# The written-out order of a gated recurrence with a convolutional gate, chosen anew

## The chip, the cores and the metric

The kernel runs on one core of a Trainium2 chip. The core has five engines with a queue each: TensorE (PE; its weight loads are listed as PEld), VectorE (DVE), ScalarE (ACT), GpSimd (POOL) and SyncE (SP), which here only issues transfers. The time is that of one execution on the device, in microseconds (us); lower is better.

## The reference

Four sequences of 6336 tokens with 256 channels go through a linear recurrence with gates, and its result `y` through a unit whose gate is a causal convolution over five tokens. Cut to what matters:

```python
sig_r, sig_i = sigmoid(r_gate), sigmoid(i_gate)
a_t = exp(8.0 * sig_r * log(clip(sigmoid(a_param), 1e-6, 1 - 1e-6)))
x_gated = sqrt(max(1.0 - a_t * a_t, 1e-6)) * sig_i * x
for t in range(S):
    h = a_t[:, t] * h + x_gated[:, t]
    y[:, t] = h
gate = sigmoid(sum(conv_w[k] * shifted(y, 4 - k) for k in range(5)))
out = (gate * (y @ w_val)) @ w_out
```

All inputs and the output are float32 in HBM.

## The kernel before

The 25344 tokens are cut into 50 windows of 512 tokens (the last has 256), and the windows into 27 chunks: chunks 0, 1 and 25 are one window of 512, chunk 26 one of 256, the others two windows each. Thus chunk c from 2 to 24 is windows 2(c-1) and 2(c-1)+1; window 48 is chunk 25, window 49 chunk 26. A half of a chunk is 128 of the 256 channels.

Each step is a small function named `op_` and two letters, and a table calls it by those letters. `ORDER` (from line 42) is one long string of such words: name, number of the window or chunk, half, and behind `@` the PSUM banks. The kernel walks through it once and emits the instructions; each engine runs its own in the order in which they come in the string, and waits in place where an input or a buffer isn't there. So the string alone fixes all queues, including SP's, on which all large transfers stand.

The words, by engine, with the line of the profile:

- SP: `lr`, `li`, `lx` load a window of r_gate, i_gate and x (L284); `st` stores a window of the output (L533); `s_wl` loads parts of the weights (L258 to L264).
- ACT: `ta`, `tb` the tangents (tanh) of a chunk of r and i (L302, L305); `ex` the exponential that makes the decays `aring` of a half (L365); `rt` the square roots of part of a batch of chunks (L398); `tg` the tangent for the gate of a window (L489); `ca` a copy of a window's result from PSUM (L522); `sa` a square (L381). Exponential and square root need different tables, and a change of table is a load on ACT (L549); `rt` come in pairs for each of eight batches, the first two batches in one go.
- POOL: `sq` the squares of the decays of a half (L373); `pp` adds one to a window of tangents (L312); `up` multiplies it with x (L324).
- DVE: `xg` multiplies with the square roots (L423, from chunk 24 on L427); `sc` the scan, that is the recurrence of a half (L470); `gv` the product of gate and value (L502); `cd` a copy of a window's result (L520); `uv` does for a window what `pp` and `up` do on POOL (L338), from x that `xp` brought to PSUM.
- PE: `tr` transposes the tangents of r (L349), `nt` the square roots (L412), `xt` the scan's input (L437); `cv` the convolution (L482), `vl` the value product (L497), `ou` the output product (L512), `xp` (L329).

A window's way is lr, ta, tr, ex, sq, rt, nt, and li, tb, pp, lx, up beside it, then xg, xt, sc, cv, tg, vl, gv, ou, a copy (ca or cd) and st. From chunk 24 on xt comes ahead of xg, and the scan reads the product from SBUF and not from PSUM: there both inputs of the scan, and both of `up`, lie in SBUF. The rings hold a few windows: four of r, i and x, so that lr.4 must wait until ta.0 has read window 0; and the eight PSUM banks are given to the steps by the words themselves. `ta` of two neighbouring chunks is transposed together (`tr` and `ex` of chunks 2, 4, 6 and so on treat that chunk and the next).

Of the kernel before, what the change touches and what calls it, by code (L numbers as in the profile page):

```python
# [47 lines left out]
lx.6 tr.4.1@2,3 tg.0 li.8 pp.5 sc.1.1 tr.4.0@4,5 ta.6 li.9 xt.2.1@7 pp.4 sc.2.1 vl.0@0,1 up.4 ex.4.0 gv.0 nt.3@6,7 up.5
ex.4.1 xt.2.0@5 cv.1@0,1 sc.2.0 sq.5.0 tb.4 ou.0.0@2,3 xg.3 vl.1@4,5 tg.1 sq.4.1 li.10 cd.0.0 xt.3.0@7 lx.9 ta.7 lr.15
cv.2@0,1 gv.1 li.11 sq.4.0 tg.2 sc.3.0 lr.17 tr.6.0@2,3 xt.3.1@4 lx.8 ex.6.0 sq.5.1 lr.14 cv.3@0,1 sc.3.1 tb.5 pp.6  # L50
tr.6.1@6,7 up.6 xp.7@2,3 uv.7 ex.6.1 li.12 lx.11 ou.1.0@4,5 cd.1.0 sq.7.0 lx.10 tg.3 st.0 xp.9@2,3 uv.9 tb.6 cv.4@0,1
sq.6.0 tg.4 li.14 vl.2@2,3 sq.6.1 li.13 gv.2 lr.16 vl.3@0,1 li.15 lx.13 gv.3 rt.2.0 vl.4@4,5 pp.8 ou.2.0@2,3 gv.4
sq.7.1 ou.3.0@0,1 cd.3.0 up.8 rt.2.1 cd.2.0 nt.4@0,1 xg.4 pp.10 lx.12 ou.4.0@2,3 st.2 pp.11 cd.4.0 xt.4.0@0 up.11
sc.4.0 nt.5@2,3 tb.7 xt.4.1@6 cv.5@4,5 up.10 lx.15 xg.5 st.1 ta.9 sc.4.1 xt.5.0@0 pp.12 nt.6@2,3 ta.8 lr.20 pp.13 lr.21
xg.6 up.13 vl.5@6,7 tb.8 lr.19 sc.5.0 lr.18 tr.8.0@2,3 li.16 xt.5.1@1 lx.14 tg.5 pp.15 li.17 li.18 ex.8.0 gv.5 up.15
st.3 tr.8.1@4,5 li.19 sc.5.1 ou.5.0@6,7 st.4 ex.8.1 up.12 nt.7@2,3 xt.6.1@0 cd.5.0 ta.11 cv.8@4,5 sq.8.1 sc.6.1 st.5
cv.6@6,7 tg.8 pp.14 tg.6 xg.7 vl.6@4,5 ta.10 sq.9.0 cv.7@0,1 gv.6 xt.6.0@7 tg.7 up.14 lr.23 sc.6.0 ou.6.0@4,5 lr.22
tb.9 lx.19 tr.10.0@0,1 lx.17 sq.9.1 vl.7@2,3 cd.6.0 ex.10.0 xt.7.0@7 gv.7 st.6 sq.8.0 vl.8@4,5 lx.18 tb.10 li.21
cv.9@0,1 gv.8 lx.16 sq.11.0 sc.7.0 tg.9 tr.10.1@2,3 li.23 ex.10.1 ou.7.0@4,5 pp.17 ou.8.0@0,1 cd.7.0 pp.16 xt.7.1@7
ta.12 cv.10@2,3 sq.10.1 cd.8.0 st.7 li.20 cv.11@4,5 lr.24 sc.7.1 tg.10 st.8 sq.10.0 lr.25 tg.11 vl.10@2,3 lr.27 gv.10  # L60
sq.11.1 vl.9@0,1 li.22 rt.3.0 gv.9 ou.10.0@6,7 up.17 cd.10.0 vl.11@2,3 cv.12@4,5 gv.11 pp.19 lx.21 rt.3.1 lr.26
ou.9.0@0,1 up.19 cd.9.0 nt.8@6,7 xg.8 st.9 ou.11.0@0,1 st.10 up.16 cd.11.0 xt.8.0@6 sc.8.0 nt.10@0,1 pp.18 tg.12 lx.20
xt.8.1@2 tb.11 up.18 sc.8.1 nt.9@6,7 ta.13 cv.13@4,5 pp.21 xg.9 pp.20 tg.13 lr.29 tr.12.1@2,3 xg.10 xt.9.1@6 lr.28
up.21 ex.12.1 li.25 cv.14@4,5 sc.9.1 lx.22 lx.23 li.24 vl.12@0,1 tg.14 sq.13.1 vl.13@2,3 tb.12 gv.12 tr.12.0@6,7
sq.12.1 gv.13 vl.14@4,5 ex.12.0 li.27 gv.14 lx.25 xt.9.0@3 li.26 pp.23 cv.15@0,1 sc.9.0 ta.14 up.20 ou.12.0@4,5 ta.15
ou.14.0@6,7 lr.31 cd.12.0 sq.12.0 nt.11@2,3 cd.14.0 tg.15 lr.33 tr.14.0@4,5 lr.30 pp.22 xg.11 ex.14.0 lr.32 ou.13.0@6,7
st.12 up.23 xt.10.0@0 cd.13.0 st.11 vl.15@2,3 lx.24 tb.13 sc.10.0 cv.17@4,5 sq.15.0 tg.17 tr.14.1@6,7 li.28 st.14 gv.15
ex.14.1 up.22 xt.10.1@4 st.13 cv.16@0,1 sc.10.1 li.29 tg.16 pp.24 vl.17@2,3 tb.14 sq.13.0 gv.17 vl.16@0,1 xt.11.1@4
gv.16 cv.19@2,3 ta.16 li.31 pp.26 lx.26 sc.11.1 li.30 pp.25 ou.16.0@6,7 ta.17 cv.18@0,1 lx.27 sq.14.1 cd.16.0 tg.19
ou.15.0@4,5 pp.27 cd.15.0 tg.18 xt.11.0@2 sq.15.1 sc.11.0 st.15 lr.34 vl.18@0,1 lr.36 rt.4.0 ou.17.0@4,5 sq.14.0 st.16  # L70
gv.18 vl.19@6,7 lr.37 gv.19 up.24 ou.18.0@0,1 lr.35 cd.17.0 rt.4.1 up.25 cd.18.0 nt.12@6,7 st.17 nt.13@2,3 xg.12 up.26
tr.16.0@4,5 lx.29 xg.13 xt.12.0@7 st.18 cv.20@0,1 sc.12.0 up.27 lx.30 tg.20 vl.20@2,3 lx.28 tb.15 gv.20 ou.19.0@0,1
cd.19.0 nt.14@6,7 ex.16.0 li.33 pp.28 li.32 tr.16.1@2,3 xg.14 pp.29 xt.12.1@1 sc.12.1 ex.16.1 cv.21@4,5 sq.17.0
xt.13.1@6 tg.21 sq.16.0 sc.13.1 ou.20.0@0,1 tb.16 cv.23@2,3 sq.16.1 xt.13.0@7 tg.23 cd.20.0 vl.21@4,5 ta.18 gv.21
sq.17.1 cv.22@0,1 sc.13.0 tg.22 lr.39 ou.21.0@2,3 pp.31 lx.31 ta.19 lr.38 up.29 vl.22@0,1 li.34 xt.14.0@5 li.35 gv.22
st.19 ca.21.0 tr.18.0@6,7 sc.14.0 cv.25@0,1 up.28 ex.18.0 st.21 st.20 lr.40 ou.22.0@2,3 lx.33 pp.30 cd.22.0 tg.25
nt.15@4,5 tb.17 sq.19.0 xt.14.1@0 xg.15 st.22 lx.32 tr.18.1@2,3 sc.14.1 ex.18.1 vl.23@6,7 up.30 cv.24@4,5 gv.23 ta.20
xt.15.1@3 up.31 lx.34 sc.15.1 vl.24@0,1 tg.24 ou.23.0@6,7 sq.18.1 tb.18 cv.26@4,5 gv.24 cd.23.0 tg.26 li.38 pp.34
ou.24.0@2,3 li.37 cd.24.0 lr.41 sq.19.1 vl.26@4,5 li.36 lx.35 gv.26 rt.5.0 vl.25@0,1 st.23 xt.15.0@3 sq.18.0 li.39
gv.25 cv.27@4,5 st.24 sc.15.0 pp.33 ou.25.0@0,1 lr.42 rt.5.1 pp.32 nt.16@6,7 lr.43 cd.25.0 up.33 ou.26.0@2,3 xg.16  # L80
cv.29@0,1 cd.26.0 up.32 xt.16.0@7 xt.16.1@6 sc.16.0 st.26 lx.37 nt.17@2,3 tg.29 pp.35 lx.36 tg.27 up.34 vl.29@0,1 xg.17
ta.21 cv.28@4,5 sc.16.1 up.35 tg.28 lr.44 tr.20.0@2,3 lr.45 ex.20.0 st.25 gv.29 nt.18@4,5 lx.39 lx.38 vl.27@6,7 xg.18
# [5 lines left out]
tb.22 st.29 sc.19.1 cv.34@4,5 lx.41 pp.40 lr.46 tg.34 lr.49 pp.41 ou.32.0@2,3 lr.48 tg.35 cd.32.0 li.45 pp.43 vl.33@6,7
li.44 gv.33 lr.47 sq.23.0 vl.35@0,1 gv.35 rt.6.0 vl.34@2,3 xt.19.0@7 up.40 gv.34 ou.33.0@0,1 sc.19.0 ou.35.0@2,3
sq.23.1 ca.35.0 ou.34.0@4,5 ca.33.0 up.41 cd.34.0 nt.20@6,7 rt.6.1 st.33 xg.20 st.32 nt.21@0,1 up.43 lx.45 xg.21  # L90
xt.20.0@7 lx.44 xt.20.1@6 li.46 sc.20.0 cv.37@2,3 li.47 pp.42 cv.36@0,1 up.42 tg.37 sc.20.1 nt.22@4,5 tg.36 xt.21.1@7
ta.25 xg.22 vl.36@0,1 tb.23 cv.38@2,3 gv.36 tr.25.1@4 xt.21.0@6 tg.38 sc.21.1 li.48 pp.45 tr.25.0@5 lx.46 ex.25.1
# [488 lines left out]
```

## Time and profile before

| | |
|---|---|
| median of 3 runs | 283.39 us (283.16 to 283.83) |
| profiled execution, its own time | 283.24 us |
| its span in the profile | 281.4 us |
| busy: PE, DVE, ACT, POOL | 242.2, 246.4, 268.2, 236.7 us |
| moved by DMA | 104.75 MB |
| mean granted TensorE clock | 0.986 |

The profile shows one execution. Its span is the time from the first to the last instruction; the execution's own time is 1.8 us longer. In a row of a timeline stand the start, the time that the row covers, the engine, the line, the operation, what it writes and reads, how many instructions the row puts together, and in brackets how long the engine stood idle before it and what released it. Where several instructions make one row, they overlap a little, so two of 1.03 us may cover 1.92.

### The profile page before, as it was taken

What the parts mean: (1) busy time and instruction counts of PE and PEld (TensorE: products, weight loads), DVE (VectorE), ACT (ScalarE), POOL (GpSimd) and SP (SyncE); (2) the same over time, 40 slices, a digit from 0 to 9 for tenths busy, and PEclk for the clock granted to TensorE, in tenths of its full rate; (3) what the DMA queues carried; (4) which work ended last, traced back from release to release, by engine and by line L of the source; (5) the groups of instructions that cost most, each with busy time, mean ns of one, the idle gap of its engine ahead of it and who ended that gap; (6) DMA issues with size and microseconds to landing.
All of it is one profiled execution on the core that took longest, in us unless ns stands there. A gap on an engine that the chain in (4) does not pass through costs nothing.

```text
span 281.4 us, 6153 instructions
## 1 busy us (share of the span) xinstructions
PE 242.2 (86%) x2465; PEld 163.6 (58%) x2465; DVE 246.4 (88%) x209; ACT 268.2 (95%) x185; POOL 236.7 (84%) x155
## 2 busy tenths in 40 slices
...
GB/s 269 412 413 404 375 408 409 409 412 360 375 401 412 416 420 413 416 408 412 419 417 417 392 321 403 419 412 419 415 415 359 415 417 376 276 263 208 148 179 257
DMA packets 29419, 104.75 MB, mean 372 GB/s; under 512 B 3271, under 2 KB 3790, under 8 KB 29390
## 3 DMA queue, kind: packets, MB, share of 16 engines
...
## 4 chain that ended last, share of the span: by engine, by line
ACT 41%; DVE 20%; issue 14%; PE 14%; DMA 7%; POOL 3%; SPq 0%; ACTq 0%; DVEq 0%
DVE yring L470 9%; ACT ering L398 9%; ACT aring L365 8%; ACT taring L302 8%; DMA rring<-in_r_gate_dram 7%; ACT tgring L489 7%; DVE tgring L502 6%; ACT tbring L305 5%; PE banks L482 4%; ACT L549 4%; PE banks L512 4%; DVE oring L520 3%; PE banks L497 3%; PE banks L349 2%; DVE uring L423 2%
## 5 line engine op out<-in xcount | busy, mean ns | idle before, releaser
L373 POOL TENSOR_TENSOR ering<-aring 128x1024 f32<-128x1024 f32 (+2 forms) x52 | 91.2, 1775 | 14.1 <-ACT aring L365 13.7
L324 POOL TENSOR_TENSOR uring<-tbring,xring 128x1024 bf16<-128x1024 bf16 (+1 forms) x46 | 97.7, 2140 | 2.7 <-DMA xring<-in_x_dram 1.7
L470 DVE TENSOR_TENSOR_SCAN yring<-aring,yring,banks 128x1024 bf16<-128x1024 f32 (+4 forms) x46 | 96.8, 2117 | 1.3 <-PE banks L437 1.0
L482 PE MATMUL banks<-yring,diag 64*64 64x512 bf16 (+7 forms) x1060 | 61.7, 365 | 2.4 <-ACT oring L522 0.8
L502 DVE SCALAR_TENSOR_TENSOR tgring<-tgring,banks 128x1024 bf16<-128x1024 bf16 (+1 forms) x50 | 58.8, 1198 | 4.7 <-PE banks L497 4.5
L312 POOL TENSOR_SCALAR tbring<-tbring 128x1024 bf16<-128x1024 bf16 (+1 forms) x46 | 47.3, 1040 | 8.8 <-ACT tbring L305 8.8
L512 PE MATMUL banks<-wo,tgring 128*128 128x256 bf16 x396 | 51.4, 274 | 3.8 <-DVE tgring L502 2.8
L497 PE MATMUL banks<-yring,wv 128*128 128x512 bf16 (+4 forms) x212 | 49.8, 365 | 3.8 <-ACT tgring L489 2.7
L365 ACT ACTIVATE aring<-banks,khf 128x2048 f32<-128x2048 bf16 (+3 forms) x32 | 52.8, 1682 | 0.4 <-PE banks L349 0.2
L489 ACT ACTIVATE tgring<-banks 128x1024 bf16<-128x1024 f32 (+1 forms) x50 | 50.0, 1019 | 2.6 <-PE banks L482 2.0
L512 PEld LDWEIGHTS <-tgring 128*128 128x128 bf16 x396 | 41.8, 114 | 14.9 <-issue 6.5
L302 ACT ACTIVATE taring<-rring 128x2048 bf16<-128x2048 f32 (+2 forms) x27 | 47.5, 1770 | 1.8 <-DMA rring<-in_r_gate_dram 1.8
L305 ACT ACTIVATE tbring<-iring 128x2048 bf16<-128x2048 f32 (+2 forms) x27 | 47.7, 1773 | 0.2
L398 ACT ACTIVATE ering<-ering 128x4096 bf16<-128x4096 f32 (+2 forms) x14 | 44.6, 3221 | 0.1
L482 PEld LDWEIGHTS <-diag 64*64 64x64 bf16 x1060 | 28.5, 106 | 27.8 <-issue 12.2
L520 DVE COPY oring<-banks 128x1024 f32<-128x1024 f32 x33 | 39.7, 1214 | 1.6 <-PE banks L512 1.2
L437 PE MATMUL banks<-ident,uring 128*128 128x128 f32 x198 | 31.0, 285 | 5.8 <-DVE uring L423 3.0
L349 PE MATMUL banks<-ident_b,taring 128*128 128x128 bf16 x396 | 29.5, 230 | 6.8 <-ACT taring L302 6.1
L412 PE MATMUL banks<-ident,ering 128*128 128x128 f32 x184 | 28.0, 296 | 6.5 <-DVE oring L520 2.5
L497 PEld LDWEIGHTS <-wv 128*128 128x128 bf16 x212 | 19.4, 97 | 23.5 <-issue 9.9
L349 PEld LDWEIGHTS <-taring 128*128 128x128 bf16 x396 | 25.6, 103 | 12.7 <-ACT taring L302 7.0
L412 PEld LDWEIGHTS banks<-ident,ering 128*128 128x128 f32 x184 | 24.7, 208 | 11.5 <-ACT ering L398 3.9
...
## 6 DMA issues: line engine op xcount, KB each, us to landing
...
```

The costliest lines, as they stand in the source:

```text
L302: nc.scalar.activation(**tangent(c, taring, NTR, rring, NRI))
L305: nc.scalar.activation(**tangent(c, tbring, NTI, iring, NII))
L324: nc.gpsimd.tensor_tensor(out=u, in0=t1, in1=xt, op=ALU.mult)
L365: nc.scalar.activation(out=dst, in_=src, func=ACT.Exp, scale=khf[:, h:h + 1], bias=khf[:, h:h + 1])
L373: nc.gpsimd.tensor_tensor(out=e, in0=a, in1=a, op=ALU.mult)
L398: nc.scalar.activation(out=ering[:].bitcast(BF16)[:, 4 * o:4 * o + 2 * n], in_=ering[:, 2 * o:2 * o + 2 * n], func=ACT.Sqrt, scale=-0.25, ...
L470: nc.vector.tensor_tensor_scan(out=yring[:, h, col:col + o1 - o0], data0=aring[:, h, a_at[c] + o0:a_at[c] + o1], data1=xT[:, o0:o1], initi ...
L482: nc.tensor.matmul(out=gp[oh * 64:oh * 64 + 64, h, a:b], lhsT=diag[half * 64:half * 64 + 64, h, k, :], rhs=yring[half * 64:half * 64 + 64, ...
L489: nc.scalar.activation(out=tgring[:, w % NTG, :, 0:wins[w]], in_=live.pop(("gp", w))[:, :, 0:wins[w]], func=ACT.Tanh, scale=0.5)
L497: nc.tensor.matmul(out=val[:, m, a:b], lhsT=wv[:, hk, m * P:(m + 1) * P], rhs=yring[:, hk, col:col + b - a], start=(hk == 0), stop=(hk == ...
L502: nc.vector.scalar_tensor_tensor(out=tgring[:, w % NTG, :, 0:wins[w]], in0=tgring[:, w % NTG, :, 0:wins[w]], scalar=1.0, in1=live.pop(("va ...
L512: nc.tensor.matmul(out=ops[:, j * D:(j + 1) * D], lhsT=gv[:, hk, j:wins[w]:J], rhs=wo[:, hk, :], start=(hk == 0), stop=(hk == H - 1))
```

## The change

In its author's words: same operations, rings and batches; order of all queues, banks and copy engines chosen anew for tangents that begin at the landing of the first transfer. `ORDER` is replaced; nothing else in the file differs. Both strings have 951 words. All steps have the same inputs, rings and batches; the sequence of words and the banks differ. Counted by engine, 79 of 169 words of ACT that occur in both stand at another place of their queue, 95 of 168 of DVE, 113 of 145 of POOL, 128 of 261 of PE and 165 of 204 of SP; most by a few places. Ten words have no counterpart: windows 4 and 8 go by xp and uv in the place of 7 and 9, window 28 is copied by ACT (`ca.28.0`) and not by DVE (`cd.28.0`), and the square of half 0 of chunk 26 is POOL's (`sq.26.0`) and not ACT's (`sa.26.0`). The diff, cut to the beginning, the words that have no counterpart, and the end:

```diff
-s_ident s_small s_kt s_diag lr.0 lr.1 lr.3 li.1 lr.2 ta.0 ta.1 lr.4 tr.0.0@4 tr.0.1@1 ex.0.0 lr.5 tr.1.1@7 tr.1.0@3
-li.0 ex.0.1 li.2 ex.1.1 lx.0 tb.1 li.3 ex.1.0 ta.2 sq.1.0 sq.1.1 lr.7 ta.3 sq.0.0 lr.6 lx.1 li.5 tb.0 lr.8 tr.2.0@0,1
-lr.9 ex.2.0 tr.2.1@4,5 lx.3 ex.2.1 lx.2 sq.3.0 xp.0@6,7 li.4 tb.2 sq.0.1 s_wl.2 sq.2.1 ta.4 s_wl.0 xp.1@4,5 sq.3.1 lx.5
-uv.1 s_wl.3 uv.0 sq.2.0 rt.0.0 s_wl.1 pp.3 rt.1.0 nt.1@5 lr.10 up.3 nt.0@3 lr.11 xg.0 xg.1 lx.4 xt.0.1@6 pp.2 li.6
+s_ident s_small s_kt s_diag lr.0 lr.1 lr.3 lr.2 li.1 ta.0 lr.4 tr.0.0@4 ta.1 tr.0.1@7 ex.0.0 lr.5 tr.1.1@6 tr.1.0@5
+li.0 lx.0 ex.1.0 li.2 ex.1.1 sq.1.0 li.3 ta.2 sq.0.0 ex.0.1 lr.6 lr.7 tb.1 sq.0.1 s_wl.3 ta.3 s_wl.0 sq.1.1 lx.1 tb.0
+tr.2.0@4,5 lr.9 ex.2.0 lr.8 tr.2.1@2,3 lx.3 ex.2.1 sq.3.0 lx.2 tb.2 xp.0@4,5 sq.2.0 uv.0 s_wl.1 li.5 s_wl.2 ta.4 sq.2.1
+xp.1@2,3 pp.2 lx.5 uv.1 li.4 sq.3.1 rt.0.0 li.6 lx.4 pp.3 rt.1.0 nt.0@4 nt.1@6 li.7 xg.0 up.3 lr.11 xg.1 xt.0.1@4
...
-gv.28 ou.27.0@2,3 tg.30 vl.30@0,1 cd.27.0 up.37 tb.20 xt.17.0@6 gv.30 ou.28.0@2,3 cv.31@4,5 cd.28.0 ta.22 li.43 up.36
+li.43 li.41 ou.28.0@0,1 sc.17.0 xt.18.1@6 li.42 tg.31 lx.40 vl.31@2,3 pp.39 ca.28.0 nt.19@4,5 gv.31 ta.23 pp.38 st.28
...
-sq.24.1 cv.41@0,1 sa.26.0 tg.42 sc.23.0 up.46 tg.41 vl.40@4,5 vl.42@2,3 gv.40 vl.41@0,1 sq.25.1 rt.7.0 gv.41 xt.24@6,7
-sq.25.0 ou.40.0@4,5 gv.42 pp.48 ca.40.0 vl.44@0,1 xg.24 up.48 rt.7.1 st.40 ou.41.0@2,3 st.38 cv.44@4,5 cd.41.0
-cv.43@6,7 sc.24.1 st.41 tg.44 cv.45@2,3 tg.43 gv.44 tb.26 vl.43@4,5 pp.49 gv.43 ou.42.0@6,7 up.49 ca.42.0 ou.44.0@0,1
-sc.24.0 ca.44.0 st.42 vl.45@4,5 tg.45 ou.43.0@6,7 xt.25@1 ca.43.0 xt.26@0 xg.25 cv.47@2,3 gv.45 st.43 st.44 cv.46@6,7
-tg.47 xg.26 sc.25.1 tg.46 vl.47@0,1 sc.25.0 ou.45.0@2,3 ca.45.0 gv.47 vl.46@6,7 cv.48@4,5 st.45 gv.46 tg.48 ou.47.0@0,1
-sc.26.1 ca.47.0 sc.26.0 vl.48@2,3 gv.48 st.47 ou.46.0@4,5 cv.49@6,7 ca.46.0 tg.49 ou.48.0@2,3 st.46 ca.48.0 vl.49@4,5
-gv.49 st.48 ou.49.0@7 ca.49.0 st.49
+sq.26.0 rt.7.0 xt.24@6,7 pp.48 ou.40.0@4,5 gv.42 sq.25.0 ca.40.0 vl.44@0,1 xg.24 up.48 rt.7.1 ou.41.0@2,3 st.40
+cv.44@4,5 cd.41.0 cv.43@6,7 sc.24.0 st.41 cv.45@2,3 tg.44 tg.43 gv.44 vl.43@4,5 gv.43 ou.42.0@6,7 ca.42.0 ou.44.0@0,1
+sc.24.1 ca.44.0 vl.45@4,5 tg.45 st.44 ou.43.0@6,7 xt.25@1 ca.43.0 cv.47@2,3 xg.25 tb.26 gv.45 st.43 cv.46@6,7 st.42
+tg.47 pp.49 sc.25.0 up.49 tg.46 vl.47@4,5 sc.25.1 vl.46@0,1 xt.26@7 xg.26 ou.45.0@2,3 gv.47 cv.48@6,7 ca.45.0 sc.26.0
+st.45 tg.48 gv.46 ou.47.0@2,3 ca.47.0 vl.48@4,5 sc.26.1 gv.48 st.47 ou.46.0@0,1 cv.49@2,3 ca.46.0 tg.49 ou.48.0@6,7
+st.46 ca.48.0 vl.49@4,5 gv.49 st.48 ou.49.0@3 ca.49.0 st.49
```

More of the change, by code (lines that the diff above doesn't have):

```diff
@@ L48 @@
[L48 to L82, printed above, removed]
@@ L88 @@
[L88 to L92, printed above, removed]
@@ new lines @@
+sc.0.1 xt.0.0@6 lr.10 up.2 sc.0.0 nt.2@2,3 xt.1.0@5 ta.5 xt.1.1@1 s_wcast lx.6 xg.2 sc.1.0 tb.3 lr.13 tr.4.1@6,7
+xt.2.0@0 lr.12 sc.1.1 ex.4.1 li.8 pp.5 sc.2.0 cv.1@2,3 li.9 lx.7 xt.2.1@5 tb.4 sq.5.1 xp.4@6,7 uv.4 tg.1 li.11 pp.6
+vl.1@0,1 li.10 ta.6 lx.8 gv.1 up.5 tr.4.0@2,3 sc.2.1 cv.0@0,1 ex.4.0 sq.4.1 nt.3@6,7 tg.0 xg.3 up.6 vl.0@2,3 ta.7 gv.0
+ou.1.0@0,1 xt.3.1@5 cd.1.0 tb.5 pp.7 cv.2@2,3 lr.17 sc.3.1 st.1 up.7 lr.16 tr.6.0@0,1 tg.2 lx.9 lr.15 ex.6.0 lr.14
+sq.4.0 xt.3.0@5 sc.3.0 tr.6.1@2,3 tb.6 sq.6.0 ou.0.0@6,7 vl.2@0,1 cd.0.0 ex.6.1 cv.4@4,5 li.15 sq.5.0 gv.2 st.0
```

54 lines of the change are left out of this document (45 added, 9 removed).

## The prediction

> **What bounds the kernel now.** I read the page's busy shares and its chain first, then the engines' busy time in three stretches, then ScalarE's waits, and at last the timelines of the first 16 us and of the last 30 us.
>
> ```profile
> span 281.4 us, 6153 instructions
> PE 242.2 (86%) x2465; PEld 163.6 (58%) x2465; DVE 246.4 (88%) x209; ACT 268.2 (95%) x185; POOL 236.7 (84%) x155
> ACT 41%; DVE 20%; issue 14%; PE 14%; DMA 7%; POOL 3%; SPq 0%; ACTq 0%; DVEq 0%
> ...
> 0.00:16.00 16.00, 5.56 (x45) 4.63 (x46) 3.63 (x19) 12.65 (x13) 4.02 (x10) 1.00 0.90 350
> 16.00:260.00 244.00, 219.82 (x2254) 147.92 (x2252) 227.65 (x175) 242.57 (x159) 230.88 (x143) 0.99 0.99 389
> 260.00:281.40 21.40, 16.80 (x170) 11.10 (x170) 15.09 (x16) 12.98 (x15) 1.79 (x2) 0.98 0.50 198
> ```
>
> In the rows of the three stretches the columns are the length and the busy time of PE, its weight loads, DVE, ACT and POOL, then clock, DMA share and GB/s. From 16 to 260 us ACT is busy for 242.57 of 244.00 us: it has 1.43 us of idle time in all. So whatever the order of work on the other engines, a new order cannot shorten this stretch by more than 1.43 us unless ACT is given less to do, and a microsecond added to ACT's queue lengthens it by up to a microsecond. DMA is as full there (0.99). In the last 21.4 us ACT is busy for only 12.98 us, so that stretch has another limit. The span divides into ACT's start, ACT's dense queue, and the tail.
>
> **The start of ACT's queue.** These are ACT's rows of the first 19 us, and below them TensorE's transposes behind the second tangent, the chain's step that ends at the fourth piece of tangents, and a later pair of tangents that had no wait.
>
> ```profile
> 4.39 1.06 ACT L302 ACTIVATE taring<-rring 128x1024 bf16<-128x1024 f32 x1 [1.36 <-DMA rring<-in_r_gate_dram]
> 5.67 1.06 ACT L302 ACTIVATE taring<-rring 128x1024 bf16<-128x1024 f32 x1 [0.23 <-DMA rring<-in_r_gate_dram]
> 6.63 2.10 ACT L365 ACTIVATE aring<-banks,khf 128x512 f32<-128x512 bf16 x3
> 8.62 1.06 ACT L305 ACTIVATE tbring<-iring 128x1024 bf16<-128x1024 f32 x1
> 9.57 0.78 ACT L365 ACTIVATE aring<-banks,khf 128x512 f32<-128x512 bf16 x1
> 10.23 3.87 ACT L302 ACTIVATE taring<-rring 128x2048 bf16<-128x2048 f32 x2
> ...
> 15.22 4.01 ACT L365 ACTIVATE aring<-banks,khf 128x2048 f32<-128x2048 bf16 x2 [0.18 <-PE banks L349]
> ...
> 6.78 1.03 PE L349 MATMUL banks<-ident_b,taring 128*128 128x128 bf16 x8 [0.25 <-ACT taring L302]
> ...
> 6.75 5.41 DMA rring<-in_r_gate_dram
> ...
> 118.63 3.73 ACT L302 ACTIVATE taring<-rring 128x2048 bf16<-128x2048 f32 x2
> ```
>
> The first tangent already begins at the landing of the first transfer (4.39 us, released by DMA), and the second at that of the second (5.67 us). The change keeps lr.0, lr.1, lr.3 as the first three loads, so neither can begin sooner; nothing is gained ahead of 6.63 us.
>
> Behind them the order was ex.0.0, ex.0.1, ex.1.1 (the three of 6.63 us), tb.1, ex.1.0, ta.2, ta.3. It becomes ex.0.0, ex.1.0, ex.1.1, ta.2, ex.0.1, tb.1, ta.3. ex.1.0 is now second, but its transposes tr.1.0 are still the last of TensorE's four groups: the eight transposes of 6.78 us are tr.1.1 and then tr.1.0, and they end at 7.81 us. ex.0.0 leaves ACT at 6.63 + 0.66 = 7.29 (three take 2.10, one takes 0.78, so each takes a place of 0.66). ACT therefore stands for some 0.53 us where it did not before. Queued behind it are ex.1.1, ta.2, ex.0.1, tb.1 and ta.3. From 7.83 us on: ex.1.0 and ex.1.1 to 9.15, ta.2 to 10.96 (a place of 3.73 - 1.91 = 1.82, by the pair of 118.63 us), ex.0.1 to 11.62, tb.1 to 12.57, and ta.3 at 12.57. Before, ta.3 began at 12.16, when lr.5 landed (6.75 + 5.41), and the pair ta.2, ta.3 took 3.87 instead of 3.73, so 0.14 us of the new wait takes the place of an old one. The first part is **+0.4 us** for everything behind it on ACT. Its bounds are 0 (tr.1.0 done when ex.0.0 ends) and +0.5 (no old wait absorbed).
>
> **Loads that move.** lr.2 goes ahead of li.1, which ta.2 needs sooner and tb.1 now needs later. The weights, lr.10 and lr.11 and the loads for iring are exchanged on SP's queue. I cost them at nothing by the page's row of GB/s, each slice being 281.4/40 = 7.035 us.
>
> ```profile
> GB/s 269 412 413 404 375 408 409 409 412 360 375 401 412 416 420 413 416 408 412 419 417 417 392 321 403 419 412 419 415 415 359 415 417 376 276 263 208 148 179 257
> ...
> 30.87 1.91 ACT L302 ACTIVATE taring<-rring 128x2048 bf16<-128x2048 f32 x1
> ```
>
> The load moved latest for its reader is li.4, now the 21st of the 0.524 MB transfers, with 0.52 MB of weights ahead: 11.5 MB. The first four slices carry 10.5 MB by 28.1 us and the fifth 0.375 MB a microsecond, so li.4 lands at about 30.8. Its reader tb.3 follows ta.5, at 30.87 + 0.4 + 1.82 = 33.1. The cover is 2.3 us; if SP issued li.4 later than that allows, tb.3 and all of ACT would pay the rest.
>
> **Work that changes engine.** The copy of window 28 goes from DVE to ACT, and the square of chunk 26, half 0, from ACT to POOL; windows 4 and 8 take the PSUM road of op_xp and op_uv where 7 and 9 took it, which is the same number of instructions on each engine. The number of pairs of square roots, and so of table loads, is the same.
>
> ```profile
> 222.30 1.92 ACT L522 COPY oring<-banks 128x1024 f32<-128x1024 f32 x2
> 249.43 0.51 ACT L381 ACTIVATE ering<-aring 128x256 f32<-128x256 f32 x1
> 249.75 2.02 ACT L489 ACTIVATE tgring<-banks 128x1024 bf16<-128x1024 f32 x2
> ...
> L373 POOL TENSOR_TENSOR ering<-aring 128x1024 f32<-128x1024 f32 x45 | 84.6, 1897 | 5.3 <-ACT aring L365 4.9 <-ACT tgring L489 0.4
> ...
> L520 DVE COPY oring<-banks 128x1024 f32<-128x1024 f32 x33 | 39.7, 1214 | 1.6 <-PE banks L512 1.2 <-ACT aring L365 0.2
> ...
> L522 ACT COPY oring<-banks 128x1024 f32<-128x1024 f32 x16 | 16.2, 1026 | 2.5 <-PE banks L512 2.5
> ...
> L373 POOL TENSOR_TENSOR ering<-aring 128x256 f32<-128x256 f32 x1 | 0.6, 632 | 0.0
> ```
>
> One copy takes ACT 1.026 us, and two in a row 1.92, so its place is 0.9 us. The square's place is 249.75 - 249.43 = 0.3 us. ACT's dense queue becomes 0.9 - 0.3 = **0.6 us** longer. DVE is relieved of 1.21 us and POOL given 0.63 us. With the 0.4 of the start, ACT reaches its last pair of square roots 1.0 us later. Bounds: -0.4, if all its 1.43 us of idle time vanished, and +2.9, if one sqrt pair had in addition to wait for a whole 1.9 us square on POOL; I take the sum, which is nearest to a queue whose idle time stays as it is.
>
> **The tail.** Rows of ACT, DVE and POOL from the last square roots, then TensorE's from the end of chunk 24.
>
> ```profile
> 253.08 1.92 ACT L398 ACTIVATE ering<-ering 128x2048 bf16<-128x2048 f32 x1
> ...
> 255.44 1.22 DVE L427 TENSOR_TENSOR uring<-banks,ering 128x2048 bf16<-128x2048 bf16 x1
> 257.79 2.34 DVE L470 TENSOR_TENSOR_SCAN yring<-aring,yring,uring 128x1024 bf16<-128x1024 f32 x1
> 262.29 2.86 DVE L470 TENSOR_TENSOR_SCAN yring<-aring,yring,uring 128x1024 bf16<-128x1024 f32 x1
> 268.36 1.27 DVE L470 TENSOR_TENSOR_SCAN yring<-aring,yring,uring 128x512 bf16<-128x512 f32 x1
> ...
> 252.52 2.06 POOL L373 TENSOR_TENSOR ering<-aring 128x512 f32<-128x512 f32 x2
> ...
> 255.68 2.16 POOL L324 TENSOR_TENSOR uring<-tbring,xring 128x1024 bf16<-128x1024 bf16 x1
> 261.84 1.17 POOL L324 TENSOR_TENSOR uring<-tbring,xring 128x512 bf16<-128x512 bf16 x1
> ...
> 264.27 0.82 PE L437 MATMUL banks<-ident,uring 128*128 128x128 f32 x6
> 265.21 2.35 PE L482 MATMUL banks<-yring,diag 64*64 64x512 bf16 x40
> 270.20 1.27 PE L482 MATMUL banks<-yring,diag 64*64 64x512 bf16 x20
> ...
> 277.86 0.59 ACT L522 COPY oring<-banks 128x512 f32<-128x512 f32 x1 [0.93 <-PE banks L512]
> ```
>
> xg.24 (255.44) follows the square root of chunk 24 (done at 255.00), with 0.44 us to spare. ACT 1.0 us later moves it by **0.6**. Then DVE scans one half of chunk 24, does two gate products and scans the other half, whose end releases cv.47 on TensorE (265.21). The second scan took 2.86 us and the first 2.34, with equal shapes; the one that was slower began while POOL's up.49 ran (261.84 to 263.01), and both read two tensors of SBUF. I read the extra 0.52 us as a wait for POOL.
>
> The Trainium skill, "SBUF — State Buffer", section "Who interferes with whom", says that a DVE instruction with two SBUF inputs and a GpSimd instruction that reads SBUF exclude each other, and that the later one waits out the whole of the earlier. By that rule the scan would have ended at 263.01 + 2.34 = 265.35; the trace has 265.15, so it agrees within 0.2 us.
>
> The change moves tb.26 behind ca.43, so up.49 no longer runs there: **-0.5 us**. POOL's up.48, which ended (257.84) as the first scan began, comes later: its queue starts with tb.24, 1.3 us later on ACT (0.4 and 0.9), and between them one 512-wide square less (2.06 for two; it is done ahead of tb.24) and the 0.63 us square more, some 0.4 us less in all. It ends at 258.7, the first scan is due at 257.79 + 0.6 = 258.4: **+0.3** (bounds 0 and 2.16, the whole of up.48). The end of chunk 24 is thus 0.4 us later than before.
>
> Behind it TensorE is packed: 5 us of cv.47, cv.46, two value products and ou.45 lie between 265.21 and 270.20, and no gap. xt.26, which before was done inside 264.27 to 265.09 while TensorE had to wait anyway, now stands between vl.46 and ou.45: two of those six transposes, **+0.3**. It waits for up.49, which now meets the scans of chunk 25 (1.27 us each, the same two SBUF inputs). If POOL starts first, between the two scans, cv.48 waits for the second scan, 1.17 us later, and for xg.26 behind it, instead of for TensorE: another **+0.35**. With no meeting it is 0; with up.49 behind both scans, TensorE stands at xt.26 until up.49 ends: +1.2. I take the middle one. From cv.48 on the order is the old one, and each step's inputs come before TensorE asks for them.
>
> Sum: 0.6 - 0.5 + 0.3 + 0.3 + 0.35 = about **+1.05 us**. The profiled execution took 283.24 us in all, its span 281.4; with the sum, 284.3. The median of the runs shown is 0.15 above it, so I predict **284.4 us**.
>
> **Rivals.**
> (1) DVE is the limit, and faster results. DVE is busy for 227.65 of the 244 us, and it loses 1.21 us of copy and 0.52 of stretched scan. If ACT recovers its idle time, DVE sets xg.24: -1.2 - 0.5 + 0.3 + 0.3 = -1.1, 282.3 us. Against it: ACT would have to be at most 0.44 us late at the last square roots, and has 0.6 us of new work. It decides as soon as ACT's lateness there falls below 0.44.
> (2) The same time. The change does not do what it says: it is chosen for tangents that begin at the first landing, and they did (4.39 us). ACT's 0.4 and 0.6 use up its 1.43 us of idle time, and the freed scan pays for the moved transposes: 283.4. For it speaks that all engines and DMA are full in the same way; against it that the idle time of ACT is spread over many small waits.
> (3) TensorE stands at xt.26 behind up.49: the place is the last 15 us, the price 1.2 instead of 0.35, the result 285.3 us. It decides once POOL finds both scans of chunk 25 ahead of it. The Trainium skill's rule above would make this wait a whole one, not a shared slowing.
> (4) A new wait inside ACT's queue: squares end on POOL just as a pair of square roots is due, and one square of 1.9 us too late gives 286.3 us. POOL is busy for 230.88 of 244 us, so it cannot catch up quickly.
>
> **How the numbers follow.** A measurement of this kernel can tell about 0.2%, 0.57 us, from no change. My forecast has 0.44 (of which 0.05 lies within 0.57 us of before), rival 1 has 0.20, rival 2 0.15, rival 3 0.10 and rival 4 0.11. Faster: 0.20. Same: 0.15 + 0.05 = 0.20. Slower: 0.39 + 0.10 + 0.11 = 0.60. The likeliest case's own range is 283.6 to 285.2, from the bounds 0 and +0.5 of the start, 0 and +1.2 of xt.26. The range for 8 in 10 goes from 282.2, just below rival 1, to 286.0, above rival 3 and the bounds of the tail; rival 4 is left out.
>
> **What would show it.** Start: an idle 0.5 us of ACT ahead of ex.1.0, near 7.3 us, and ex.2.0 at 15.6. Middle: ACT's idle time from 16 to 260 us still near 1.4, the square root of chunk 24 at 254.1. Tail: both scans of chunk 24 near 2.3 us, one of chunk 25 or up.49 held up, and TensorE idle ahead of cv.48. I am wrong if ACT's idle in the middle falls below 0.5 us, if it rises by 2 or more, or if the last square roots come no later than before.

## The result, and the profile after

| | before | changed |
|---|---|---|
| median, timed side by side on one chip (11 runs each) | 282.82 us (282.23 to 283.83) | 284.17 us (283.84 to 284.99) |
| ratio, 95% interval | | 1.0054 [1.0042, 1.0065] |
| profiled execution, its own time | 283.24 us | 284.65 us |
| its span | 281.4 us | 282.8 us |
| mean granted TensorE clock | 0.986 | 0.993 |

The changed kernel is slower by 0.54%, some 1.5 us (1.2 to 1.8); between the profiled executions lie 1.41 us. The first lines are from the page of the changed kernel: span, busy shares, chain and ACT's two tangent lines (after the bar: busy time, mean ns of one; then idle time ahead of them and its releaser).

```profile
span 282.8 us, 6114 instructions
PE 239.4 (85%) x2438; PEld 164.9 (58%) x2465; DVE 246.1 (87%) x208; ACT 268.3 (95%) x185; POOL 238.2 (84%) x156
POOL 32%; DMA 22%; ACT 19%; issue 13%; DVE 5%; PE 4%; SPq 2%; POOLq 1%; ACTq 0%; DVEq 0%
...
L302 ACT ACTIVATE taring<-rring 128x2048 bf16<-128x2048 f32 (+2 forms) x27 | 47.9, 1781 | 2.3 <-DMA rring<-in_r_gate_dram 2.3
...
L305 ACT ACTIVATE tbring<-iring 128x2048 bf16<-128x2048 f32 (+2 forms) x27 | 48.0, 1782 | 1.0 <-DMA iring<-in_i_gate_dram 0.9
```

DMA's share of the chain went from 7% to 22%, and POOL's from 3% to 32%. The chain follows only one of several full queues: in the view of waits ACT waits for POOL in neither kernel, so POOL's share by itself shows no cost. On the page of before the same two lines end so:

```profile
L302 ACT ACTIVATE taring<-rring 128x2048 bf16<-128x2048 f32 (+2 forms) x27 | 47.5, 1770 | 1.8 <-DMA rring<-in_r_gate_dram 1.8
L305 ACT ACTIVATE tbring<-iring 128x2048 bf16<-128x2048 f32 (+2 forms) x27 | 47.7, 1773 | 0.2
```

ACT stands 1.3 us longer for loads of r and i. These are the stretches of the changed kernel (columns as in the prediction), and then ACT's timeline where it stood for a load behind the start:

```profile
16.00:260.00 244.00, 216.07 (x2219) 148.67 (x2245) 225.99 (x174) 241.81 (x158) 230.42 (x143) 0.99 0.99 388
260.00:282.80 22.80, 18.09 (x188) 11.88 (x182) 16.46 (x16) 14.15 (x16) 2.69 (x2) 0.99 0.48 193
```

```profile
37.55 1.91 ACT L305 ACTIVATE tbring<-iring 128x2048 bf16<-128x2048 f32 x1 [0.71 <-DMA iring<-in_i_gate_dram]
...
231.81 1.91 ACT L305 ACTIVATE tbring<-iring 128x2048 bf16<-128x2048 f32 x1 [0.24 <-DMA iring<-in_i_gate_dram]
...
239.70 1.91 ACT L302 ACTIVATE taring<-rring 128x2048 bf16<-128x2048 f32 x1 [0.77 <-DMA rring<-in_r_gate_dram]
```

From 16 to 260 us ACT now has 244.00 - 241.81 = 2.19 us of idle time, where it had 1.43. Of it 0.71 + 0.24 + 0.77 = 1.72 us are three waits for loads, and only 0.47 is left of all the small waits. The first wait is tb.4's for li.7, the second tb.23's for li.44 and li.45, the last ta.24's for lr.46 and lr.47. The timeline of SP's queue in the changed kernel shows why the last pair was late:

```profile
216.70 0.55 SPq L284 DMA_DIRECT2D iring<-in_i_gate_dram  x1
217.30 7.58 SPq L533 DMA_DIRECT2D out_dram<-oring  x3
224.93 1.18 SPq L284 DMA_DIRECT2D rring<-in_r_gate_dram  x1
...
228.83 0.44 SPq L284 DMA_DIRECT2D rring<-in_r_gate_dram  x1
```

SP comes to the stores of windows 29, 32 and 34 at 217.30 and stands there (by the view of waits 6.0 us of it for one copy of DVE's). Behind them stands lr.46, issued at 224.93, and after li.44, three other loads and a store comes lr.47 at 228.83. In the kernel before, lr.46 was the first of three loads at 215.35 and lr.47 left at 219.67.

ACT's start, in the timeline of the changed kernel:

```profile
4.32 1.06 ACT L302 ACTIVATE taring<-rring 128x1024 bf16<-128x1024 f32 x1 [1.30 <-DMA rring<-in_r_gate_dram]
...
7.76 1.45 ACT L365 ACTIVATE aring<-banks,khf 128x512 f32<-128x512 bf16 x2 [0.46 <-PE banks L349]
...
15.55 4.01 ACT L365 ACTIVATE aring<-banks,khf 128x2048 f32<-128x2048 bf16 x2 [0.18 <-PE banks L349]
```

ACT stands 0.46 us for TensorE ahead of ex.1.0, and ex.2.0 begins 0.33 us later than before (15.22). The tail, rows of ACT, DVE, POOL and PE from four timelines of the changed kernel:

```profile
254.26 1.91 ACT L398 ACTIVATE ering<-ering 128x2048 bf16<-128x2048 f32 x1
...
258.81 2.34 DVE L470 TENSOR_TENSOR_SCAN yring<-aring,yring,uring 128x1024 bf16<-128x1024 f32 x1
...
263.31 2.35 DVE L470 TENSOR_TENSOR_SCAN yring<-aring,yring,uring 128x1024 bf16<-128x1024 f32 x1
...
267.83 3.31 DVE L470 TENSOR_TENSOR_SCAN yring<-aring,yring,uring 128x512 bf16<-128x512 f32 x2
...
256.74 2.15 POOL L324 TENSOR_TENSOR uring<-tbring,xring 128x1024 bf16<-128x1024 bf16 x1
...
268.00 2.07 POOL L324 TENSOR_TENSOR uring<-tbring,xring 128x512 bf16<-128x512 bf16 x1
...
265.83 2.36 PE L482 MATMUL banks<-yring,diag 64*64 64x512 bf16 x40
...
271.36 1.42 PE L482 MATMUL banks<-yring,diag 64*64 64x512 bf16 x20
...
279.23 0.59 ACT L522 COPY oring<-banks 128x512 f32<-128x512 f32 x1 [0.92 <-PE banks L512]
```

The second scan of chunk 24 is free (2.35 us, was 2.86). up.49 now runs between the two scans of chunk 25: it covers 2.07 us where it took 1.17, and the two scans cover 3.31 us where two of 1.27 would cover some 2.5. Taken one by one, the first scan has 1.28 us, as before, and the second, from 269.02 us on, 2.12. From the last square roots to the last copy it is 279.23 - 254.26 = 24.97 us; before, 277.86 - 253.08 = 24.78.

### The profile page after: what moved, and what is told of

It reads as the page before. It is cut to its first block, busy times and chain, and to the rows that moved or that the text cites. A ratio compares the mean times of both kernels' runs of the same rounds, so it can differ in the third digit from the quotient of the medians.

```text
span 282.8 us, 6114 instructions
## 1 busy us (share of the span) xinstructions
PE 239.4 (85%) x2438; PEld 164.9 (58%) x2465; DVE 246.1 (87%) x208; ACT 268.3 (95%) x185; POOL 238.2 (84%) x156
## 4 chain that ended last, share of the span: by engine, by line
POOL 32%; DMA 22%; ACT 19%; issue 13%; DVE 5%; PE 4%; SPq 2%; POOLq 1%; ACTq 0%; DVEq 0%
POOL ering L373 14%; POOL uring L324 11%; DMA xring<-in_x_dram 8%; DMA rring<-in_r_gate_dram 8%; POOL tbring L312 6%; ACT aring L365 5%; ACT taring L302 4%; ACT tgring L489 4%; DMA iring<-in_i_gate_dram 4%; ACT tbring L305 3%; DMA out_dram<-oring 3%; DVE tgring L502 3%; SPq L284 2%; PE banks L512 2%; ACT ering L398 1%
## 5 line engine op out<-in xcount | busy, mean ns | idle before, releaser
L512 PE MATMUL banks<-wo,tgring 128*128 128x256 bf16 x396 | 50.7, 274 | 4.4 <-DVE tgring L502 3.2
L497 PE MATMUL banks<-yring,wv 128*128 128x512 bf16 (+7 forms) x185 | 47.0, 363 | 2.4 <-ACT tgring L489 0.6
L482 PEld LDWEIGHTS <-diag 64*64 64x64 bf16 x1060 | 30.7, 106 | 25.6 <-issue 10.4
L520 DVE COPY oring<-banks 128x1024 f32<-128x1024 f32 x32 | 38.3, 1213 | 2.2 <-PE banks L512 1.4
L412 PE MATMUL banks<-ident,ering 128*128 128x128 f32 x184 | 27.4, 296 | 6.2 <-ACT ering L398 3.2
L423 DVE TENSOR_TENSOR uring<-banks,uring 128x2048 bf16<-128x2048 bf16 (+1 forms) x24 | 27.8, 1170 | 3.6 <-PE banks L412 3.2
```

The lines of the kernel that those rows point to most:

```text
L482: nc.tensor.matmul(out=gp[oh * 64:oh * 64 + 64, h, a:b], lhsT=diag[half * 64:half * 64 + 64, h, k, :], rhs=yring[half * 64:half * 64 + 64, ...
L497: nc.tensor.matmul(out=val[:, m, a:b], lhsT=wv[:, hk, m * P:(m + 1) * P], rhs=yring[:, hk, col:col + b - a], start=(hk == 0), stop=(hk == ...
L512: nc.tensor.matmul(out=ops[:, j * D:(j + 1) * D], lhsT=gv[:, hk, j:wins[w]:J], rhs=wo[:, hk, :], start=(hk == 0), stop=(hk == H - 1))
```

## The experiments

Each kernel was timed beside the kernel before on the same chip; ratios are to it, with 95% intervals. Kernels that change only the order compute what the reference does. In some of them the lines of the file stand one further down.

**The start alone undone.** In the changed kernel tr.1.0 goes ahead of tr.1.1.

```diff
-tr.0.1@7 ex.0.0 lr.5 tr.1.1@6 tr.1.0@5 li.0
+tr.0.1@7 ex.0.0 lr.5 tr.1.0@5 tr.1.1@6 li.0
```

> The changed order with tr.1.0 ahead of tr.1.1 on TensorE, so that the transposes which the second exponential needs are no longer the last of four. Theory A (ScalarE's queue is the clock up to the last square roots, each idle time in it is paid in full): the 0.46 us idle ahead of ex.1.0 falls below 0.05, ex.2.0 begins 0.3 to 0.4 us sooner than 15.55, and the time falls by 0.3 to 0.45 us against the changed kernel (from about 1.4 us above the kernel before to about 1.0 above). Theory B (loads set the pace behind the start, a sooner start only makes ScalarE wait longer for li.7 at 37.5 us): the idle time at the start goes, the wait at 37.5 grows from 0.71 to about 1.1 us, and the time stays within 0.15 us.

Measured: 284.46 us, ratio 1.0074 [1.0049, 1.0099]. From ACT's timeline of this kernel:

```profile
15.23 4.01 ACT L366 ACTIVATE aring<-banks,khf 128x2048 f32<-128x2048 bf16 x2 [0.19 <-PE banks L350]
...
37.05 1.91 ACT L306 ACTIVATE tbring<-iring 128x2048 bf16<-128x2048 f32 x1 [0.52 <-DMA iring<-in_i_gate_dram]
...
232.03 1.92 ACT L306 ACTIVATE tbring<-iring 128x2048 bf16<-128x2048 f32 x1 [1.00 <-DMA iring<-in_i_gate_dram]
```

ACT gets its 0.3 us back at 15.23, and no time is won. It arrives earlier at tb.4 and stands there for li.7 until 37.05; in a second profile of the changed kernel (below), with the late start, tb.4 began at 37.04 without a wait. The wait at 37 us did not grow to the 1.1 us of theory B, but the one near 232 us grew from 0.24 to 1.00. So the 0.4 us of the start is not what makes the changed kernel slow.

**The copy of window 28 given back to DVE.**

```diff
-pp.39 ca.28.0 nt.19@4,5
+pp.39 cd.28.0 nt.19@4,5
```

> The changed order with window 28 copied by VectorE again. Theory A (ScalarE's queue is the clock): one copy of 1.02 us with a place of 0.9 us leaves ScalarE, the square roots of chunk 24 (254.26) come 0.9 us sooner and the time falls by 0.7 to 0.9 us. Theory B (ScalarE only had its waits moved; VectorE and the loads are as tight): the later wait for lr.47 at 239.7 us grows from 0.77 to about 1.6 us or VectorE's 1.21 us comes back, and the time falls by less than 0.2 us or rises by up to 1.2.

Measured: 285.08 us, 1.0094 [1.0080, 1.0107], slower still. ACT's timeline of this kernel has

```profile
205.08 1.01 ACT L523 COPY oring<-banks 128x1024 f32<-128x1024 f32 x1 [1.15 <-PE banks L513]
```

The next copy on ACT, ca.30, waits 1.15 us for ou.30, which needs the PSUM banks that window 28's result leaves; DVE frees them later than ACT did. So in the changed order the 0.9 us can't be had back by the exchange alone; the experiment replaced a cost by a wait and doesn't price the copy.

**The same copy given to ACT in the kernel before.**

```diff
-cv.31@4,5 cd.28.0 ta.22
+cv.31@4,5 ca.28.0 ta.22
```

> The order of before with window 28 copied by ScalarE: the change's one added piece of ScalarE work, alone. Theory A (ScalarE's queue is the clock up to the last square roots; the prediction's 0.9 us): 0.7 to 0.9 us above the kernel before. Theory E (a copy moved off VectorE pays for itself, since VectorE is as full around 200 us; the run with the copy put back did not get faster): from 0.9 us below to 0.2 above.

Measured: 283.45 us, 1.0028 [1.0014, 1.0041]: +0.8 us (0.4 to 1.2). In the old order one copy more on ACT costs about its place of 0.9 us, as theory A had it: ACT's way from the table load ahead of rt.5 to the one behind rt.6, which holds this copy, takes 52.01 us, and 51.24 to 51.26 in four other profiles of the old order.

**The tail, both ways.** The changed kernel with the words of before behind rt.7.0, and the kernel before with the words of the changed one there (st.38, which is still to be issued at that place, follows st.40):

```diff
-rt.7.0 xt.24@6,7 pp.48 ou.40.0@4,5 gv.42 sq.25.0
+rt.7.0 xt.24@6,7 sq.25.0 ou.40.0@4,5 gv.42 pp.48
...
-rt.7.0 gv.41 xt.24@6,7 sq.25.0 ou.40.0@4,5 gv.42 pp.48
+rt.7.0 gv.41 xt.24@6,7 pp.48 ou.40.0@4,5 gv.42 sq.25.0
...
```

> The changed order up to rt.7.0 and the order of before from there on (tb.26 early, xt.26 ahead of cv.47). Prediction's theory (the freed scan brings 0.5 us, the two moved transposes and the meeting of up.49 with the scans of chunk 25 cost 0.27 plus 0.35 to 1.2): the second scan of chunk 24 is 2.86 us again, cv.48 begins at about +0.6 less, and the time changes by -0.1 to -0.7 us. Rival (the tail is as long either way, all of the loss stands ahead of 254 us): within 0.1 us of the changed kernel.

> The order of before up to rt.7.0 and the changed order from there on: the mirror of the run above. If the tail costs what the run above gives back, the time is 0.1 to 0.7 us above the kernel before; if all of the loss stands ahead of the last square roots, it is within 0.1 us of the kernel before.

Measured: the changed kernel with the old tail 283.81 us, 1.0059 [1.0035, 1.0084], no gain that could be told from none. The kernel before with the new tail 283.06 us, 1.0021 [1.0010, 1.0032]: +0.6 us (0.3 to 0.9). In the traces, the time from rt.7.0 to the last copy is 24.78 us in both kernels with the old tail and 24.97 and 25.14 in the two with the new one (24.97 to 25.43 in the five other profiles with it). The new tail costs 0.2 to 0.6 us, the smaller part of the loss.

**up.49 early in the kernel before**, that is, the shared stretch of the second scan taken away alone:

```diff
-sc.24.1 st.41 tg.44 cv.45@2,3 tg.43 gv.44 tb.26 vl.43@4,5 pp.49 gv.43
+sc.24.1 st.41 tb.26 pp.49 tg.44 cv.45@2,3 tg.43 gv.44 vl.43@4,5 gv.43
```

> The order of before with tb.26 and pp.49 ahead of tg.44, so that up.49 ends before the second scan of chunk 24 begins. Theory P (the scan's extra 0.52 us is a wait for POOL's read of SBUF, and this scan sets the tail): both scans 2.34 us, up.49 over before 262, the time 0.3 to 0.5 us below the kernel before. Rival (the scan is long for another reason, or TensorE is the limit there): the second scan stays near 2.86 us, or the time stays within 0.15 us or rises by up to 0.6 us as tg.44 and tg.43 are 0.55 us later.

Measured: 282.84 us, 1.0008 [0.9999, 1.0017]. DVE's timeline of this kernel, then POOL's:

```profile
257.66 2.34 DVE L470 TENSOR_TENSOR_SCAN yring<-aring,yring,uring 128x1024 bf16<-128x1024 f32 x1
...
262.38 2.34 DVE L470 TENSOR_TENSOR_SCAN yring<-aring,yring,uring 128x1024 bf16<-128x1024 f32 x1
265.24 0.69 DVE L427 TENSOR_TENSOR uring<-banks,ering 128x1024 bf16<-128x1024 bf16 x1 [0.52 <-PE banks L437]
...
260.50 1.17 POOL L324 TENSOR_TENSOR uring<-tbring,xring 128x512 bf16<-128x512 bf16 x1
```

With up.49 out of its way the second scan takes 2.34 us, so the 0.52 us was indeed its wait for POOL. But the next DVE step then waits 0.52 us for TensorE, and nothing is won. Part of that is the edit's own doing: tg.44 and tg.43 now stand behind tb.26, TensorE stands 0.26 us for one of them, and cv.47 begins 12.30 us after rt.7.0 where it began 12.13 after it. So the run doesn't price the freed scan alone. A bound can be read: in this run, with the scan long done, cv.47 begins 0.75 us behind the start of xt.25 and xt.26 (264.50 and 265.25), in the kernel before 0.94 us behind it (264.27 and 265.21). As long as xt.26 stands in front of cv.47, the freed scan is worth 0.2 us at most.

**The late loads.** First the changed kernel was profiled once more, as a partner for the next:

> The changed order itself once more, on the same chip as the three kernels beside it, as their measure. Both theories: 1.0 to 1.7 us above the kernel before, ScalarE waiting for loads near 37, 232 and 240 us for some 1.8 us in all.

Measured: 284.03 us, 1.0047 [1.0034, 1.0061]. In this execution tb.4 did not wait for li.7, but ta.24 stood 1.02 us: these are 1.0 us of waits for loads in place of the expected 1.8. Then lr.46, lr.47 and li.44 were issued ahead of the stores of windows 32 and 34, and li.7 ahead of lx.4:

```diff
-li.6 lx.4 pp.3 rt.1.0 nt.0@4 nt.1@6 li.7 xg.0
+li.6 li.7 lx.4 pp.3 rt.1.0 nt.0@4 nt.1@6 xg.0
...
-li.45 st.29 sq.22.1
+li.45 li.44 st.29 lr.46 lr.47 sq.22.1
...
```

> The changed order with four loads earlier on SP's queue: li.7 ahead of lx.4, li.44 behind li.45, lr.46 and lr.47 ahead of st.32 and st.34, whose copies SP stood waiting for from 217 to 225 us. Theory C (the loss ahead of the last square roots is three new waits of ScalarE for loads, 0.71 + 0.24 + 0.77 us): these waits go, the square roots of chunk 24 begin 1.0 to 1.7 us sooner and the time falls by 0.8 to 1.6 us, close to the kernel before. Theory D (all queues are full alike and a wait that is taken away turns up elsewhere): the three waits go but others of at least 1 us come, on loads of x or i that were put behind or on the oring's stores, and the time falls by less than 0.3 us.

Measured: 284.04 us, 1.0050 [1.0036, 1.0063], no gain. Both waits are gone, but ACT's timeline has a new one, for a store:

```profile
227.16 1.01 ACT L522 COPY oring<-banks 128x1024 f32<-128x1024 f32 x1 [0.73 <-DMA out_dram<-oring]
```

Here st.29 was put behind li.44, and its landing frees the output buffer that ca.33 wants. ACT came to rt.7.0 only 0.36 us earlier than in the changed kernel (253.40 against 253.76), and from there to the last copy it took 25.43 us. That stretch is 0.46 us longer than in the changed kernel, all of it behind 274 us (0.19 us at ou.46, the rest at the last copy); what made it so stayed open. The next kernel keeps li.7 where the change has it, and puts st.29 ahead of lx.42:

```diff
-st.30 sc.19.1 sq.23.0 lx.42
+st.30 sc.19.1 sq.23.0 st.29 lx.42
...
-li.45 st.29 sq.22.1
+li.45 li.44 lr.46 lr.47 sq.22.1
...
```

> The changed order with st.29 ahead of lx.42, li.44 behind li.45, and lr.46 and lr.47 ahead of st.32 and st.34: the run of the earlier loads again, with the store that a copy of ScalarE then waited for (0.73 us) put first. Theory C (between the tables of rt.6 and of rt.7 ScalarE lost 1.0 to 1.2 us to the late landing of lr.46 and lr.47, and that is the largest part of the loss): from the table load behind rt.6 to the one ahead of rt.7 24.0 us instead of 25.2, no wait over 0.3 us between, and the time 0.8 to 1.2 us below the changed kernel (0.2 to 0.6 above the kernel before). Theory D (full queues: a wait taken away comes back elsewhere): less than 0.4 us.

Measured: 283.00 us, 0.9997 [0.9978, 1.0016]. SP's timeline of this kernel:

```profile
217.59 1.00 SPq L284 DMA_DIRECT2D iring<-in_i_gate_dram  x2
218.64 1.01 SPq L284 DMA_DIRECT2D rring<-in_r_gate_dram  x2
219.75 4.78 SPq L533 DMA_DIRECT2D out_dram<-oring  x2
```

SP still stands at the stores, but with lr.46 and lr.47 in front of them. The loss is gone. The place can be read off ACT's timelines: the table loads ahead of rt.5, behind rt.6 and ahead of rt.7, in the kernel before, in the changed kernel (the two profiles of the result), and in this kernel.

```profile
176.49 1.28 ACT L549 ACT_TABLE_LOAD   x1
...
227.75 1.28 ACT L549 ACT_TABLE_LOAD   x1
...
251.78 1.28 ACT L549 ACT_TABLE_LOAD   x1
```

```profile
176.15 1.28 ACT L549 ACT_TABLE_LOAD   x1
...
227.82 1.28 ACT L549 ACT_TABLE_LOAD   x1
...
252.96 1.28 ACT L549 ACT_TABLE_LOAD   x1
```

```profile
175.77 1.28 ACT L549 ACT_TABLE_LOAD   x1
...
227.46 1.28 ACT L549 ACT_TABLE_LOAD   x1
...
251.37 1.28 ACT L549 ACT_TABLE_LOAD   x1
```

Ahead of rt.5 the changed order is as far as the old one: the 0.32 us that it was late at the first table load (23.17 against 22.85) is gone by then. From the load behind rt.6 to the one ahead of rt.7 the old order takes 24.03 us, the changed one 25.14, and the one with the earlier loads 23.91. The 1.1 us lie in this stretch, which holds the waits of 0.24 and 0.77 us for li.44 and lr.47, and they go with the late loads. The other profiles agree: 24.02 to 24.04 us in four of the old order, 24.74 to 25.80 in four with the late loads, 23.90 to 23.91 in three with the earlier ones. Since li.44 and st.29 were moved along with lr.46 and lr.47, the run shows the price of the loads together, not of each.

The mirror of it, lr.46 and lr.47 behind the stores of windows 33 and 32 in the kernel before:

```diff
-lx.41 pp.40 lr.46 tg.34
+lx.41 pp.40 tg.34
...
-st.33 xg.20 st.32 nt.21@0,1
+st.33 xg.20 st.32 lr.46 lr.47 nt.21@0,1
```

> The order of before with lr.46 and lr.47 put behind st.33 and st.32 on SP's queue, as the changed order has them: the late loads alone. Theory C: ScalarE waits for them ahead of ta.24 by 0.5 us or more, and the time rises by 0.5 to 1.2 us. Theory D: no wait over 0.2 us ahead of ta.24, the time within 0.3 us of the kernel before.

Measured: 282.56 us, 0.9995 [0.9981, 1.0010]. The two loads left between 225.1 and 227.2 us and ta.24 didn't wait. So the mirror failed as a test: in the changed kernel lr.47 leaves only at 228.83, and the old order still had time to spare at 227. Late issue costs nothing until the cover is used up.

**All repairs at once:** the changed kernel with tr.1.0 first, li.7 ahead of lx.4, the loads of the last but one kernel, and the old tail.

```diff
-lr.5 tr.1.1@6 tr.1.0@5 li.0
+lr.5 tr.1.0@5 tr.1.1@6 li.0
...
-li.6 lx.4 pp.3 rt.1.0 nt.0@4 nt.1@6 li.7 xg.0
+li.6 li.7 lx.4 pp.3 rt.1.0 nt.0@4 nt.1@6 xg.0
...
-st.30 sc.19.1 sq.23.0 lx.42
+st.30 sc.19.1 sq.23.0 st.29 lx.42
...
-li.45 st.29 sq.22.1
+li.45 li.44 lr.46 lr.47 sq.22.1
...
```

> The changed order with all repairs: tr.1.0 ahead of tr.1.1, li.7 ahead of lx.4, the loads and st.29 of the run above, and the order of before from rt.7.0 on. Theory C: what stays is window 28's copy on ScalarE, partly paid; the time is within 0.4 us of the kernel before, perhaps below it, and 1.0 to 1.5 us below the changed kernel. Theory D: it stays 0.8 us or more above the kernel before.

Measured: 282.62 us, 0.9998 [0.9985, 1.0012]: as fast as the kernel before, not faster. ACT's timeline of this kernel shows the next wait, now for lr.10, which li.7 had been moved past:

```profile
39.64 1.91 ACT L302 ACTIVATE taring<-rring 128x2048 bf16<-128x2048 f32 x1 [0.51 <-DMA rring<-in_r_gate_dram]
```

To remove it, lr.11 and lr.10 were put ahead of lx.4 as well:

```diff
-li.6 li.7 lx.4 pp.3
+li.6 li.7 lr.11 lr.10 lx.4 pp.3
...
```

> The repaired order of the run before with lr.11 and lr.10 also ahead of lx.4, so that neither tb.4 nor ta.6 waits for a load near 37 to 40 us (0.51 us there). Theory C (a wait of ScalarE early in its full queue is paid at the end): the wait goes and the time falls by 0.3 to 0.5 us, below the kernel before. Theory D (an early wait is absorbed, since the loads hold ScalarE at the same pace later, or xp.4 now waits for lx.4): within 0.2 us of the run before.

Measured: 286.39 us, 1.0124 [1.0101, 1.0147]. Rows of PE's and ACT's timelines of this kernel:

```profile
39.80 3.61 PE L329 MATMUL banks<-xring,ident 128*128 128x512 f32 x4 [3.03 <-DMA xring<-in_x_dram]
...
45.24 2.06 ACT L365 ACTIVATE aring<-banks,khf 128x2048 f32<-128x2048 bf16 x1 [4.15 <-PE banks L349]
```

lx.4 now lands late, TensorE stands 3.03 us at xp.4, the transposes tr.4 stand behind it, and ACT stands 4.15 us at the exponential that needs them. Two loads put ahead of one cost 3.5 us, which neither theory had.

## Why the prediction was right, and where it was not

The direction holds, and the median came 0.2 us below the one forecast. The way to it was partly another.

**The start (+0.4).** Shown where it was forecast: 0.46 us of idle time at 7.3 us, ex.2.0 at 15.55 for 15.6. But it isn't paid: without it tb.4 stood 0.52 us for li.7 and began as late as with it (37.05 and 37.04 us), and its removal won nothing.

**"Loads that move ... I cost them at nothing."** This is the step that failed. It followed one load, li.4, to its reader, and that one indeed brought no wait. It didn't follow lr.46, lr.47 and li.44, and it reckoned the landing by bytes alone, not by what SP must wait for ahead of a load. Nor was li.4 the load moved latest for its reader: by the same bytes li.7, the 24th transfer, lands at some 35.0 us and tb.4 is due at 36.9, a cover of 1.9 us and not 2.3, and in the first profile it let tb.4 begin only at 37.55. ACT stands 0.77 and 1.02 us at ta.24 in the two profiles of the changed kernel, the stretch around it is 1.1 us longer, and with earlier loads the changed kernel goes from 1.0047 [1.0034, 1.0061] to 0.9997 [0.9978, 1.0016]. It is the largest term of all.

**The copy and the square (+0.6).** With the start, the forecast had ACT 1.0 us late at the last square roots. With the earlier loads it comes to the table load ahead of them at 251.37 us, within the 250.80 to 251.79 of four profiles of the old order: no lateness can be told there. The copy's part is shown: from the table load ahead of rt.5 to the one behind rt.6 the changed order takes 51.67 to 51.70 us in the seven profiles that have the copy and no wait for a store, and the old one 51.24 to 51.26 in four. The copy is all that ACT has to do more there, so some 0.4 of its 0.9 us was paid, against 0.76 in the old order. Of the 1.43 us of small waits only 0.47 are left in the changed kernel (2.19 - 1.72), in line with rival 2, "use up its 1.43 us of idle time". The forecast of 254.1 us for the last square roots fitted (254.26) by luck: the late loads took the place of what was not paid.

**The tail (+0.05 with all its parts).** The scan was freed as forecast, and up.49 went between the scans of chunk 25, the middle of the three cases. The expected meeting of up.48 with the first scan did not come: the scan begins at 258.81, 0.08 us ahead of up.48's end, and has its 2.34 us. From rt.7.0 to cv.47, with xt.26 gone from in front of it, it is 11.57 us (before 12.13), so the 0.5 us of the freed scan was won up to there. To cv.48 it is 17.10 us (before 17.12): xt.26 and the meeting behind cv.47 cost 0.54 of the forecast 0.65 and took the gain back. cv.48's row is 0.15 us longer, and the last copy comes 0.2 us later.

The table loads share out the 1.41 us between the two profiled executions. Ahead of rt.5 the changed kernel is 0.34 us early; to the load behind rt.6 it takes 0.41 us more (the copy), to the one ahead of rt.7 1.11 (the loads), and from there to the last copy 0.19 (the tail): 1.37 us in all. The last three come back in the other profiles (0.4, 0.7 to 1.8, and 0.2 to 0.65 us), but the first is not a saving that the runs show: four profiles of the old order come to rt.5's table load between 175.54 and 176.50 us. The forecast's 1.05 had no loads in it and too much of the start and the copy; that the two errors nearly cancelled was luck. The kernel with the earlier loads has all the other parts and lies between 0.6 us below and 0.45 us above the kernel before: by that, too, the +1.05 was not there without the loads.

**Rivals.** Rival 1 fell: DVE did get 1.7 us of relief, and ACT set the last square roots. Rival 2's mechanism was at work, but hidden by the loads. Rivals 3 and 4 did not come: xt.26 did begin at up.49's end (270.12 against 270.07 us), but by the rows of TensorE it stood for some 0.1 us there and not for 1.2, and no row shows ACT's square roots waiting for POOL. None of the three signs of error came: ACT's idle time rose by 0.76 us, not by 2, and the square roots came later. So the signs were too wide to show the step that failed; "still near 1.4" was missed (2.19).

The rule of the Trainium skill, "SBUF — State Buffer", section "Who interferes with whom", that such DVE and GpSimd instructions exclude each other in full, fits both ways here. The first scan of chunk 25 would end at 267.83 + 1.27 = 269.10; up.49, begun at 268.00, ends at 270.07, its own 1.17 behind that within 0.2 us; and the second scan ends at 271.14, 1.27 behind up.49 within 0.2 us. That the first scan is not lengthened (1.28 us) speaks against a shared slowing.
